# A router whose second phase starts one step early, with a new table of pauses and one code per token

## The chip, the cores and the metric

The kernel runs on one core of a Trainium2 chip. The metric is device time in microseconds (us) of one execution. Below, PE is TensorE (matmuls), DVE is VectorE, ACT is ScalarE, POOL is GpSimd, and SP is SyncE, which here issues transfers and reads a register.

## What is computed

Three stages follow one another on 2304 tokens of width 512: causal attention mixed with a small memory (4 batches, 8 heads, 576 positions, 64 wide), a mixture of 8 experts, and a dense layer with the activation h * tanh(softplus(h)). The change lies in the second stage, and what runs beside it. Cut to what matters:

```
def moe(x, w_gate, w1, w2):               # x [2304, 512], E = 8, cap = 288
    logits = x @ w_gate                   # [2304, 8]
    order = argsort(-logits.flatten())
    assigned[:] = -1; counts[:] = 0
    for idx in order:                     # greedy, largest logit first
        tok, e = idx // E, idx % E
        if assigned[tok] >= 0 or counts[e] >= cap:
            continue
        assigned[tok] = e; counts[e] += 1
    for e in range(E):
        mask = assigned == e
        out[mask] = maximum(x[mask] @ w1[e], 0) @ w2[e]

def dense(x, w_in, w_out):                # 512 -> 2048 -> 512
    h = x @ w_in
    return (h * tanh(softplus(h))) @ w_out
```

## The kernel before

**The router.** The greedy assignment is sequential over 18432 logits, but only eight times does an expert fill up. So the router (class `Router`) works in eight phases. In a phase every token that is still free looks at its best expert that is not full, and a search finds the largest threshold at which some expert fills up. That expert's 288 tokens are then final. The order in which experts fill is the order in which they are computed: "expert k" in this document is the one that phase k closes, and its number is known to the program only at run time (`eid`).

The search (method `search`) fixes the threshold in six steps of 5 or 6 bits. In a step DVE compares every token's best logit with 32 or 64 candidate thresholds (tile `cm`), 18 small matmuls count the tokens of each expert above each threshold (PE `rt<-oh,cm`, L715; `oh` is a one-hot of each token's best expert), DVE turns the counts into an indicator (`ge`, `ind`), and one more matmul adds the indicators up, the vote (PE `rt<-ind,ones`, L730). After the search come a count per expert (L608), the number of the expert (`em`, `eid`), a 0/1 mark of its tokens (`bt`, with a matmul at L637), each token's place in the expert's list (L647, L648), and, in three pieces, the list of token numbers (DVE `ohp`, PE L676, then `idx`). After phase 0 the matmul engine has nothing but the router to do until the first tokens are there.

**The experts.** For expert k, three indirect transfers issued by POOL fetch its 288 rows (`xg<-xd,idx`, L993), 12 matmuls against the identity turn them (L1005), and ACT and DVE split them into a high and a low half (`xt`, L1012 and L1014). Then come the matmuls at L1021: each product is made in three passes (high x high, low x high, high x low), and the matrices are 288 tokens wide. `h<-xt,wf` and `acc<-act,wf` are the expert's two layers, `h<-y,wa` and `acc<-act,wb` the first half of the dense layer for the same tokens. Expert weights are streamed: SP loads 256 KB pieces (`raw<-moe_w`) once `eid` is known, ACT rounds each (L952, L954), and a POOL transfer that adds completes the low half (`wf<-raw`, L960). There are 5 buffers of raw pieces and 7 of finished ones. The second half of the dense layer, for all experts, comes after the last phase.

**What sets the order.** The order of instructions on PE and on POOL is the order in which the program issues them. DVE, ACT and SP are ordered by a scheduler in the compiler. The program issues the matmuls of the experts from a list (`plan`), and at places between groups of 6 or 12 matmuls calls `slot()`. A slot advances each of several background generators by one step: the router (`routing`), the loads, the gathers (`tokens`), the evacuations. A generator that yields n is called again after n slots. `Router.wait(i)` looks that n up in the table `WAIT`; entry 1 is the pause between a step's comparison and its matmuls, entry 0 that before the vote, entry 3 that before the matmul on `bt`, entry 5 that between the pieces of the list. The third row is used while the router is not further than two phases ahead of the expert being computed (`done <= cur + X["AH"]`); in the order as built, phase k+2 runs while expert k or k+1 is computed, so that row is the one in force.

`tokens(k)` issues the gather as soon as phase k is done and the tokens before it are turned, then lets `X["TW"]` = 18 slots pass and turns in four pieces with pauses between. When the plan comes to expert k first (`up1` sets `hold`), the pauses are skipped and what is left is turned at once. Phase 1 may not begin before the first group of expert 0 has been issued (`while k and not done1[0]`).

Of the kernel before, what the change touches and what calls it, by code (L numbers as in the profile page):

```python
# [466 lines left out]
NEG = -1.0e30  # L467
STEPS = ((64, 26), (64, 20), (32, 15), (32, 10), (32, 5), (32, 0))

WAIT = ((1, 2, 2, 3, 1, 4), (1, 3, 2, 2, 1, 3), (1, 1, 2, 2, 1, 2))  # L470
NTOK, E, CAP, NJ = 2304, 8, 288, 18
G, GP = 3, 96

# [71 lines left out]
class Router:  # L545
# [3 lines left out]
    def __init__(self, tc, C, cp, rp, ps, L):  # L549
        self.nc, self.C, self.rp, self.ps, self.L = tc.nc, C, rp, ps, L  # L550
        self.tc = tc
        nc = self.nc
        self.crow = cp.tile([128, E], F32, name="crow")
        nc.vector.memset(self.crow, float(CAP))
        self.pen = cp.tile([128, NJ], F32, name="pen")
        nc.vector.memset(self.pen, 0.0)
        self.A = cp.tile([128, NJ, E], BF, name="Aoh")
        nc.vector.memset(self.A, 0.0)
        self.idx = cp.tile([GP, E, G], I32, name="idx")
        self.eid = cp.tile([128, E], I32, name="eid")  # L560
        self.known = self.done = self.busy = 0
        self.mark, self.cur = None, 0

    def wait(self, i):
        return WAIT[2 if self.done <= self.cur + X["AH"] else self.busy][i]

    def after(self):

# [4 lines left out]

    def phase(self, k):
        nc, C, rp = self.nc, self.C, self.rp
        L, pen, crow, A = self.L, self.pen, self.crow, self.A
        last = k == E - 1
        bj = lambda a, n: a[:, :, None].to_broadcast([128, a.shape[1], n])
        m = rp.tile([128, NJ], F32, name="m")
# [5 lines left out]
        mu = rp.tile([128, NJ], F32, name="mu")  # L585
# [3 lines left out]
        mx = rp.tile([128, NJ], F32, name="mx")  # L589
        nc.vector.tensor_reduce(mx, w, axis=AX.X, op=OP.max)  # L590
        oh = rp.tile([128, NJ, E], BF, name="oh")
        nc.vector.tensor_tensor(oh, w, bj(mx, E), op=OP.is_equal)
        yield 1
        gg = rp.tile([128, 2, NJ], BF, name="gg")
        if last:
            for a in range(2):
                nc.vector.tensor_scalar(gg[:, a], mu, NEG / 2, None, op0=OP.is_ge)
        else:
            cut = yield from self.search(mu, oh)
            for a, op in enumerate((OP.is_ge, OP.is_gt)):  # L600
                nc.vector.tensor_scalar(gg[:, a], mu, cut, None, op0=op)

        Z = rp.tile([128, 2, NJ, E], BF, name="Z")
        for a in range(2):
            nc.vector.tensor_tensor(Z[:, 1 - a], oh, bj(gg[:, a], E), op=OP.mult)
        yield self.wait(2)
        p = self.mm()
        nc.tensor.matmul(p[:, 0:2 * NJ * E], C["ones"], Z.rearrange("p a j e -> p (a j e)"), start=True, stop=True)  # L608

        nc.vector.tensor_add(A, A, Z[:, 0])  # L610
        yield 1
        cnt = rp.tile([128, 2, E], F32, name="cnt")
        nc.vector.tensor_reduce(cnt, p[:, 0:2 * NJ * E].rearrange("p (a j e) -> p a e j", a=2, j=NJ),
                                axis=AX.X, op=OP.add)
        nc.vector.tensor_sub(Z[:, 1], Z[:, 1], Z[:, 0])
        es = rp.tile([128, E], F32, name="es")
        em = rp.tile([128, 1], F32, name="em")
        nc.vector.tensor_tensor(es, cnt[:, 1], crow, op=OP.is_ge)
        yield 1
        nc.vector.tensor_sub(crow, crow, cnt[:, 0])  # L620
        nc.vector.tensor_tensor(es, es, C["pref"], op=OP.mult)
        nc.vector.tensor_reduce(em, es, axis=AX.X, op=OP.max)
        nc.vector.tensor_scalar(es, es, em, None, op0=OP.is_equal)
        nc.vector.tensor_scalar(self.eid[:, k:k + 1], em, -1.0, float(E), op0=OP.mult, op1=OP.add)
        self.known = k + 1
        yield 1
        q = rp.tile([128, 2, NJ, E], BF, name="q2")
        eb = es[:, None, :].to_broadcast([128, NJ, E])
        nc.vector.tensor_tensor(q[:, 0], A, eb, op=OP.mult)
        nc.vector.tensor_tensor(q[:, 1], Z[:, 1], eb, op=OP.mult)  # L630
        yield 1
        bt = rp.tile([128, 2 * NJ], BF, name="bt")
        with nc.allow_low_precision("sums of one-hot entries"):
            nc.vector.tensor_reduce(bt, q.rearrange("p a j e -> p (a j) e"), axis=AX.X, op=OP.add)
        yield self.wait(3)
        p = self.mm()
        nc.tensor.matmul(p[0:36, 0:128], bt, C["ones"], start=True, stop=True)  # L637
# [8 lines left out]
        p = self.mm()  # L646
# [20 lines left out]
        p = None  # L667
        for c in range(4):
# [4 lines left out]
            if c:  # L673
                p = p or self.mm()
                for j in range(6 * c - 6, 6 * c):
# [6 lines left out]
                                                   op1=OP.add)  # L682
# [11 lines left out]
    def search(self, mu, oh):  # L694

        nc, C, rp = self.nc, self.C, self.rp
        cut = t = None
        for s, (T, sh) in enumerate(STEPS):
# [9 lines left out]
            for c in range(parts):  # L708
                j = slice(n * c, n * c + n)
# [18 lines left out]
            yield self.wait(0)  # L728
            p = self.mm()
            nc.tensor.matmul(p[:, 0:1], C["ones"][0:T, :], ind[0:T], start=True, stop=True)  # L730
            yield 1
            t = rp.tile([128, 1], I32, name="xt", bufs=2)
            if s == 0:
# [80 lines left out]
def moe(tc, ctx, C, xd, L, w1, w2, w32, whl, convert, out):  # L814
# [43 lines left out]
    def until(cond):  # L858
        while not cond():
            slot()  # L860
# [257 lines left out]

    def routing():
        for k in range(E):  # L1120
            while k and not done1[0]:
                yield 1
            yield from R.phase(k)

# [11 lines left out]

    def up1(k, f):
        until(lambda: R.done > k)
        hold[0] = ROUTE
        until(lambda: k in xts)  # L1140
        x = xts[k].get()
        hold[0] = None
        hs[k, f] = up(weight("wf", (k, 0, f)), x, relu)
        used["wf"] += 1
        done1[0] += 1
        slot()
# [67 lines left out]

    downs, ys, gs, fetched = {}, {}, {}, {}
    for u, c, k, f in plan:
        R.busy, R.cur = int(c > 1), k
# [27 lines left out]

X = {"MO": ("PE", "Pool"), "P": 4, "P0": 4, "L1": 2, "RX": 0, "XB": 2, "LAG": 6, "TW": 18, "TS": 2, "LD": 8,
     "LG": 2, "RAWB": 5, "WFB": 7, "ACTB": 12, "GB": 7, "NG": 4, "CL": (0, 1.5, 1, 2, 3, 4), "C0": 2,
     "CW": 2, "FW": 3, "FE": 4, "AH": 2, "PE": 300, "PR": 300, "PC": 600}


def program(tc, q, k, v, M_prev, z_prev, beta, w_gate, w1, w2, w_in, w_out, out):
# [54 lines left out]
```

## Time and profile before

| | us |
|---|---|
| median of 3 runs (lowest to highest) | 1119.19 (1118.27 to 1119.87) |
| the profiled execution, its own time | 1112.46 |
| its span, first to last instruction | 1110.7 |
| PE busy | 1006.2 (91% of the span) |
| DVE busy | 655.5 (59%) |
| ACT busy | 680.6 (61%) |
| POOL busy | 343.9 (31%) |

The median is 0.6% above the profiled execution; the rows below are all from that execution. Attention takes the first 307 us, phase 0 of the router the next 30, the seven other phases run beside the experts until about 740 us, and from there on the dense layer runs alone. A busy share is an average over these stages. Idle time on an engine matters where PE waits for it.

### The profile page before, as it was taken

The numbers are of one execution on the slowest core, as the hardware profiler recorded it, in microseconds if no ns is written. First come the engines' busy times: TensorE is split into PE (matmuls) and PEld (weight loads), VectorE is DVE, ScalarE is ACT, GpSimd is POOL, SyncE is SP. The second block draws the span as 40 slices with busy tenths as digits, with TensorE's granted clock in tenths as the row PEclk, the third lists the DMA queues.
The fourth block names the chain that finished last, engine by engine and source line by source line (L and its number), as shares of the span: only waits on it lengthen the run. The fifth ranks groups of instructions, "written<-read, shape, count | busy, mean of one in ns | idle before, by whom it ended". The sixth has DMA issues, their size and how long they took to land.

```text
span 1110.7 us, 22438 instructions
## 1 busy us (share of the span) xinstructions
PE 1006.2 (91%) x8088; PEld 930.1 (84%) x8088; DVE 655.5 (59%) x1986; ACT 680.6 (61%) x1632; POOL 343.9 (31%) x468
## 2 busy tenths in 40 slices
PE   5999899999926969989899987899999999999995
PEld 4778788788815969878888987899999999999995
DVE  6887878776563565665684765666652543333332
ACT  5576667677504583654755846648473976666662
POOL 5677566675204232404223334220000001111112
PEclk9899999999956979989899999999999999999998
DMA  7889988897099876958939949565536312222201
GB/s 172 218 208 235 241 204 218 227 237 184 19 331 205 197 183 168 223 131 188 232 100 229 232 99 229 169 170 174 171 98 209 125 65 86 87 86 86 76 23 43
DMA packets 177488, 182.61 MB, mean 164 GB/s; under 512 B 90912, under 2 KB 131904, under 8 KB 175328
## 3 DMA queue, kind: packets, MB, share of 16 engines
q1 hardware_dynamic: 157152, 134.59, 42.3%
q0 software_dynamic: 20224, 46.58, 19.4%
q8 instruction: 64, 1.05, 0.4%
q14 instruction: 48, 0.39, 0.1%
HBM read 97.17 MB, written 36.18 MB: 120 GB/s over the span
## 4 chain that ended last, share of the span: by engine, by line
PE 65%; DVE 10%; ACT 9%; DMA 9%; issue 3%; SPq 1%; POOL 1%; POOLq 0%; ACTq 0%; DVEq 0%
PE acc L1021 22%; PE h L1021 22%; PE o L367 4%; DMA raw<-moe_w 3%; PE pt L341 3%; DMA wf<-raw 2%; PE s L309 2%; PE o L390 2%; PE o L359 2%; PE rt L715 2%; PE s L313 2%; ACT L1095 2%; PE o L363 1%; ACT U L1095 1%; DVE H L1099 1%
## 5 line engine op out<-in xcount | busy, mean ns | idle before, releaser
L1021 PE MATMUL acc<-act,wb 128*128 128x288 f32 x1536 | 236.1, 304 | 2.3 <-DVE act L1102 2.3
L1021 PEld LDWEIGHTS acc<-act,wb 128*128 128x128 f32 x1536 | 217.5, 193 | 4.1 <-DVE act L1102 3.7
L1099 DVE TENSOR_TENSOR H<-H,U 128x288 f32<-128x288 f32 x128 | 57.0, 455 | 160.5 <-ACT U L1095 160.4
L960 POOL DMA_DIRECT2D wf<-raw x93 | 82.3, 912 | 219.4 <-ACT wf L954 122.6
L952 ACT CAST wf<-raw 128x512 fp32r<-128x512 f32 x128 | 79.1, 618 | 85.5 <-DMA raw<-moe_w 65.9
L1021 PE MATMUL h<-xt,wf 128*128 128x288 f32 x768 | 124.4, 309 | 3.4 <-DVE xt L1014 3.4
L1021 PE MATMUL acc<-act,wf 128*128 128x288 f32 x768 | 119.9, 307 | 0.0
L1021 PEld LDWEIGHTS h<-xt,wf 128*128 128x128 f32 x768 | 110.7, 197 | 9.6 <-issue 5.0
L1021 PE MATMUL h<-xt,wa 128*128 128x288 f32 x768 | 114.2, 297 | 1.3 <-DVE wa L963 1.0
L1021 PE MATMUL h<-y,wa 128*128 128x288 f32 x768 | 114.6, 302 | 0.0
L1188 POOL DMA_INDIRECT out<-xg,idx x24 | 24.3, 1011 | 288.0 <-ACT xg L1185 287.4
L1021 PEld LDWEIGHTS acc<-act,wf 128*128 128x128 f32 x768 | 108.4, 194 | 2.0 <-issue 1.4
L1021 PEld LDWEIGHTS h<-y,wa 128*128 128x128 f32 x768 | 105.8, 191 | 3.6 <-issue 3.0
L1021 PEld LDWEIGHTS h<-xt,wa 128*128 128x128 f32 x768 | 105.3, 188 | 2.5 <-DVE wa L963 1.6
L1086 ACT ACTIVATE U<-h 128x288 f32<-128x288 f32 x128 | 53.2, 416 | 81.2 <-PE h L1021 79.8
L342 ACT COPY T<-pt 128x512 f32<-128x512 f32 (+3 forms) x128 | 57.6, 455 | 63.4 <-PE pt L341 62.8
L325 ACT ACTIVATE P<-s,nm 128x576 f32<-128x576 f32 (+4 forms) x160 | 84.2, 535 | 8.1 <-DVE nm L323 6.2
L1062 ACT ACTIVATE act<-h 128x288 fp32r<-128x288 f32 x64 | 26.0, 406 | 103.0 <-PE h L1021 102.1
L341 PE MATMUL pt<-ident,P 128*128 128x128 f32 x400 | 70.4, 283 | 0.6 <-DVE T L342 0.3
L1064 DVE SCALAR_TENSOR_TENSOR act<-h,act 128x288 fp32r<-128x288 f32 x64 | 29.0, 454 | 63.9 <-ACT act L1062 60.7
L367 PE MATMUL o<-T,vm 128*64 128x128 f32 x640 | 64.9, 290 | 0.0
L309 PE MATMUL s<-k,q 128*128 128x288 f32 (+3 forms) x192 | 60.1, 350 | 2.4 <-ACT P L325 1.4
(237 smaller groups left out, 2058.2 us busy)
## 6 DMA issues: line engine op xcount, KB each, us to landing
raw<-moe_w SPq DMA_DIRECT2D x128, 256.0 KB, 4.3
wf<-raw POOLq DMA_DIRECT2D x93, 256.0 KB
k<-kh SPq DMA_DIRECT2D x60, 160.0 KB, 3.7
yd<-y SPq DMA_DIRECT2D x8, 1152.0 KB, 8.0
xt<-yd SPq DMA_DIRECT2D x8, 1152.0 KB, 5.2
whl<-parts SPq DMA_DIRECT2D x16, 512.0 KB, 5.5
part<-o SPq DMA_DIRECT2D x8, 576.0 KB, 4.0
wf<-part SPq DMA_DIRECT2D x16, 288.0 KB, 3.2
```

The source lines that it names most:

```text
L309: nc.tensor.matmul(vw[h][:, a:e], q1[:, h, r], k1[:, h, kb[h] + a:kb[h] + e], start=True, stop=False, skip_group_check=True)
L325: nc.scalar.activation(P[:, h * w:(h + 1) * w], vw[h][:, 0:w], AF.Exp, bias=nm[:, h:h + 1], scale=1.0, accum_out=den[:, h:h + 1])
L341: nc.tensor.transpose(t[:, j * 128:(j + 1) * 128], P[:, (c + j) * 128:(c + j + 1) * 128], ident)
L342: (nc.scalar.copy if eng else nc.vector.tensor_copy)(T[:, c:c + m], t[:, 0:m * 128].rearrange("p (a b) -> p a b", b=128))
L367: nc.tensor.matmul(o[s, 0:n], vm[:, j - 1 if h else 4 - j, h, :], T[:, i + j if h else i - j, 0:n], start=False, stop=(j == i), skip_group ...
L952: nc.scalar.copy(dst[:, 0], t)
L960: nc.gpsimd.dma_start(dst[:, 1].bitcast(F32), t, accum_op=OP.add)
L1021: nc.tensor.matmul(p, w[:, a, c * 128:(c + 1) * 128], x(b), start=first and i == 0, stop=last and i == 2)
L1064: nc.vector.scalar_tensor_tensor(h.t[:, 1], p[:, 0:CAP], 0.0, h.t[:, 0], op0=OP.max, op1=OP.subtract)
L1086: s = nc.scalar.activation(U, p[:, 0:CAP], AF.Sigmoid, scale=-1.0)
L1095: s = nc.scalar.activation(U, U, AF.Sin, scale=-2.0, bias=half_pi[:, 0:1])
L1099: nc.vector.tensor_mul(H, H, U)
```

## The change

Three things are changed. Phase 1 of the router may be issued without waiting for expert 0, and expert 0 waits until phase 1 has cast its first vote (a new counter, `votes`). The table of pauses has two rows instead of three, chosen by the number of finished phases alone. And tokens carry a code (the best expert's preference number, in `at`) that is compared once with the chosen expert's, where one-hot rows of 8 were multiplied and summed (`A`, `Z`, `q`).

```
-WAIT = ((1, 2, 2, 3, 1, 4), (1, 3, 2, 2, 1, 3), (1, 1, 2, 2, 1, 2))
+WAIT = ((1, 2, 2, 2, 1, 3), (1, 1, 2, 2, 1, 2))
...
     def wait(self, i):
-        return WAIT[2 if self.done <= self.cur + X["AH"] else self.busy][i]
+        return WAIT[self.done <= 1][i]
...
-            for a, op in enumerate((OP.is_ge, OP.is_gt)):
-                nc.vector.tensor_scalar(gg[:, a], mu, cut, None, op0=op)
         Z = rp.tile([128, 2, NJ, E], BF, name="Z")
-        for a in range(2):
-            nc.vector.tensor_tensor(Z[:, 1 - a], oh, bj(gg[:, a], E), op=OP.mult)
+        ops = (OP.is_ge, OP.is_ge if last else OP.is_gt)
+        for a, op in enumerate(ops):
+            nc.vector.scalar_tensor_tensor(Z[:, 1 - a], bj(mu, E), cut, oh, op0=op, op1=OP.mult)
         yield self.wait(2)
         p = self.mm()
         nc.tensor.matmul(p[:, 0:2 * NJ * E], C["ones"], Z.rearrange("p a j e -> p (a j e)"), start=True, stop=True)
-        nc.vector.tensor_add(A, A, Z[:, 0])
+        for a, op in enumerate(ops):
+            nc.vector.tensor_scalar(gg[:, a], mu, cut, None, op0=op)
+        nc.vector.tensor_mul(sure, gg[:, 1], mx)
+        nc.vector.tensor_mul(at[:, 1], gg[:, 0], mx)
+        nc.vector.tensor_sub(at[:, 1], at[:, 1], sure)
+        nc.vector.tensor_add(at[:, 0], at[:, 0], sure)
...
-        nc.vector.tensor_sub(Z[:, 1], Z[:, 1], Z[:, 0])
...
+        nc.vector.tensor_scalar(bt, at.rearrange("p a j -> p (a j)"), em, None, op0=OP.is_equal)
...
-        yield 1
-        nc.vector.tensor_tensor(q[:, 0], A, eb, op=OP.mult)
-        nc.vector.tensor_tensor(q[:, 1], Z[:, 1], eb, op=OP.mult)
-        yield 1
-            nc.vector.tensor_reduce(bt, q.rearrange("p a j e -> p (a j) e"), axis=AX.X, op=OP.add)
         yield self.wait(3)
...
             nc.tensor.matmul(p[:, 0:1], C["ones"][0:T, :], ind[0:T], start=True, stop=True)
+            self.votes += 1
...
     def routing():
         for k in range(E):
-            while k and not done1[0]:
+            while k > 1 and not done1[0]:
                 yield 1
             yield from R.phase(k)
...
     def up1(k, f):
         until(lambda: R.done > k)
+        if (k, f) == (0, 0):
+            until(lambda: R.votes > len(STEPS))
         hold[0] = ROUTE
```

Three places on PE show what this moves. **Where expert 0 begins.** Before, PE's rows from the last piece of phase 0's list (L676) on:

```order
L676 LDWEIGHTS ohp
L676 MATMUL rt<-gc,ohp 96x6
L676 LDWEIGHTS ohp
L676 MATMUL rt<-gc,ohp 96x6
L1005 MATMUL h<-ident_63,xg 128x96 x12
L1021 MATMUL h<-xt,wf 128x288 x36
L715 LDWEIGHTS cm
```

After, at the same place (L714 is the old L715, L729 the vote): the last two of the 18 matmuls of phase 1's first step, its vote, then the tokens.

```order
L714 LDWEIGHTS cm
L714 MATMUL rt<-oh,cm 64x8
L714 LDWEIGHTS cm
L714 MATMUL rt<-oh,cm 64x8
L729 LDWEIGHTS ones
L729 MATMUL rt<-ind,ones 128x1
L1005 MATMUL h<-ident_63,xg 128x96 x12
L1021 MATMUL h<-xt,wf 128x288 x18
L714 LDWEIGHTS cm
```

One step has moved in front of the turning of expert 0's tokens, and the second step stands after 18 matmuls of expert 0 where the first stood after 36.

**Where expert 1 begins.** Before, from the last matmul of phase 1's list (L676) to the turning of expert 1's tokens (L1005):

```order
L676 MATMUL rt<-gc,ohp 96x6
L1021 MATMUL acc<-act,wb 128x288 x6
L1021 MATMUL h<-y,wa 128x288 x12
L1021 MATMUL acc<-act,wb 128x288 x12
L1005 MATMUL h<-ident_63,xg 128x96 x12
L1021 MATMUL h<-xt,wf 128x288 x12
L715 LDWEIGHTS cm
```

After, the rows behind the same last matmul (now L675) of phase 1:

```order
L675 MATMUL rt<-gc,ohp 96x6
L675 LDWEIGHTS ohp
L675 MATMUL rt<-gc,ohp 96x6
L1021 MATMUL h<-y,wa 128x288 x48
L714 LDWEIGHTS cm
```

and, behind that step of phase 2, the rows up to its next step:

```order
L1021 MATMUL h<-y,wa 128x288 x6
L1021 MATMUL acc<-act,wb 128x288 x6
L729 LDWEIGHTS ones
L729 MATMUL rt<-ind,ones 128x1
L1021 MATMUL acc<-act,wb 128x288 x6
L1021 MATMUL h<-y,wa 128x288 x12
L1021 MATMUL acc<-act,wb 128x288 x6
```

then 18 matmuls of that next step, 6 of `acc<-act,wb`, and the turning of the tokens. So 30 matmuls stood between the end of phase 1 and the turning of expert 1's tokens, and now 48 + 6 + 6 + 6 + 12 + 6 + 6 = 90 do, with two router steps.

**Where expert 4 begins.** After the change, from the end of a step of phase 5:

```order
L714 MATMUL rt<-oh,cm 32x8
L1021 MATMUL acc<-act,wf 128x288 x6
L1005 MATMUL h<-ident_63,xg 128x96 x12
L1021 MATMUL h<-xt,wf 128x288 x6
L729 LDWEIGHTS ones
L729 MATMUL rt<-ind,ones 128x1
L1021 MATMUL h<-xt,wf 128x288 x6
```

Before, expert 4's 12 turning matmuls stood in four groups of 3 with matmuls between; now they are one block, 90 matmuls behind the end of phase 4. Expert 5's are one block too (102 behind). Expert 2's, which were a group of 3 and a block of 9 before, are four groups of 3 now.

## Rows read from the trace of the kernel before

**Rows 1.** The page: PE's busy tenths and granted clock in 40 slices.

```profile
PE   5999899999926969989899987899999999999995
PEclk9899999999956979989899999999999999999998
```

**Rows 2.** Windows, 400 to 412 us: busy time by engine, granted clock, DMA.

```profile
400.00:412.00 12.00, 4.63 (x23) 3.37 (x22) 7.58 (x21) 10.97 (x24) 8.87 (x10) 0.72 0.98 209
```

**Rows 3.** PE's waits, 336 us to the end: total us, times, longest.

```profile
PE rt L676 <- DVE ohp L671: 10.6, 3, 6.4
PE h L1005 <- DMA xg<-xd,idx: 9.1, 5, 4.5
PE rt L730 <- DVE ind L727: 8.3, 6, 3.7
...
PE rt L637 <- DVE bt L634: 3.9, 4, 2.0
PE h L1021 <- DVE xt L1014: 3.4, 2, 2.8
PE rt L715 <- DVE oh L592: 3.4, 1, 3.4
PE rt L715 <- DVE cm L710: 2.4, 4, 1.3
```

**Rows 4.** PE's timeline where expert 1 begins: start, us, what, idle before.

```profile
396.68 0.39 PE L676 MATMUL rt<-gc,ohp 128*96 128x6 bf16 x6
...
399.39 1.78 PE L1021 MATMUL acc<-act,wb 128*128 128x288 f32 x12
405.67 0.39 PE L1005 MATMUL h<-ident,xg 96*128 96x96 f32 x1 [4.50 <-DMA xg<-xd,idx]
408.37 0.42 PE L1005 MATMUL h<-ident,xg 96*128 96x96 f32 x1 [2.31 <-DMA xg<-xd,idx]
409.33 2.15 PE L1005 MATMUL h<-ident,xg 96*128 96x96 f32 x10 [0.54 <-DMA xg<-xd,idx]
411.46 3.25 PE L1021 MATMUL h<-xt,wf 128*128 128x288 f32 x12
...
415.69 3.25 PE L1021 MATMUL acc<-act,wb 128*128 128x288 f32 x12
```

**Rows 5.** PE's timeline: a first step of phase 0, and expert 0's turning.

```profile
310.11 1.12 PE L715 MATMUL rt<-oh,cm 128*64 128x8 bf16 x18 [4.48 <-DVE oh L592]
...
341.48 0.39 PE L1005 MATMUL h<-ident,xg 96*128 96x96 f32 x1 [5.02 <-issue]
...
344.02 2.14 PE L1005 MATMUL h<-ident,xg 96*128 96x96 f32 x10 [0.96 <-DMA xg<-xd,idx]
```

**Rows 6.** DVE's timeline in phase 0, from the expert's number to its mark.

```profile
328.75 0.16 DVE L622 TENSOR_REDUCE em<-es 128x1 f32<-128x8 f32 x1
...
329.78 0.45 DVE L634 TENSOR_REDUCE bt<-q 128x36 bf16<-128x288 bf16 x1
```

**Rows 7.** PE's timeline where expert 2 begins.

```profile
485.53 0.91 PE L1005 MATMUL h<-ident,xg 96*128 96x96 f32 x9
489.20 1.06 PE L1021 MATMUL h<-xt,wf 128*128 128x288 f32 x6 [2.76 <-DVE xt L1014]
...
491.61 1.64 PE L1021 MATMUL acc<-act,wb 128*128 128x288 f32 x6
```

**Rows 8.** ACT and DVE near 527 us, and shares of the waiting chain, 336 to 740.

```profile
526.92 0.62 ACT L952 CAST wf<-raw 128x512 fp32r<-128x512 f32 x1 [4.28 <-DMA raw<-moe_w]
...
528.40 0.46 DVE L1064 SCALAR_TENSOR_TENSOR act<-h,act 128x288 fp32r<-128x288 f32 x1 [6.98 <-ACT act L1062]
...
by line: PE acc L1021 22.8%; PE h L1021 21.9%; DMA raw<-moe_w 9.3%; DMA wf<-raw 6.8%; PE rt L715 3.5%; issue 3.4%; DVE H L1099 3.0%; ACT L1095 2.9%; ACT wf L952 1.7%; ACT wf L954 1.6%; ACT U L1095 1.5%; ACT U L1086 1.5%; DVE ohp L671 1.4%; 
```

**Rows 9.** Windows over two gather instructions of POOL, columns as in rows 2.

```profile
635.79:641.34 5.55, 3.68 (x28) 3.45 (x26) 5.40 (x15) 5.17 (x12) 5.55 (x1) 1.00 0.34 101
337.87:341.81 3.94, 0.33 (x1) 0.18 (x1) 1.73 (x4) 0.00 (x0) 3.33 (x4) 0.50 0.30 86
```

More of the change, by code (lines that the diff above doesn't have):

```diff
@@ L556, in __init__ @@
         nc.vector.memset(self.pen, 0.0)
-        self.A = cp.tile([128, NJ, E], BF, name="Aoh")
-        nc.vector.memset(self.A, 0.0)
+        self.at = cp.tile([128, 2, NJ], F32, name="at")
+        nc.vector.memset(self.at, 0.0)
         self.idx = cp.tile([GP, E, G], I32, name="idx")
         self.eid = cp.tile([128, E], I32, name="eid")
-        self.known = self.done = self.busy = 0
-        self.mark, self.cur = None, 0
+        self.known = self.done = 0
+        self.votes = 0
+        self.mark = None
     def wait(self, i):
-        return WAIT[2 if self.done <= self.cur + X["AH"] else self.busy][i]
+        return WAIT[self.done <= 1][i]
     def after(self):
@@ L575, in phase @@
         nc, C, rp = self.nc, self.C, self.rp
-        L, pen, crow, A = self.L, self.pen, self.crow, self.A
+        L, pen, crow, at = self.L, self.pen, self.crow, self.at
         last = k == E - 1
@@ L593, in phase @@
         yield 1
-        gg = rp.tile([128, 2, NJ], BF, name="gg")
-        if last:
-            for a in range(2):
-                nc.vector.tensor_scalar(gg[:, a], mu, NEG / 2, None, op0=OP.is_ge)
-        else:
+        cut = NEG / 2
+        if not last:
             cut = yield from self.search(mu, oh)
-            for a, op in enumerate((OP.is_ge, OP.is_gt)):
-                nc.vector.tensor_scalar(gg[:, a], mu, cut, None, op0=op)
         Z = rp.tile([128, 2, NJ, E], BF, name="Z")
-        for a in range(2):
-            nc.vector.tensor_tensor(Z[:, 1 - a], oh, bj(gg[:, a], E), op=OP.mult)
+        ops = (OP.is_ge, OP.is_ge if last else OP.is_gt)
+        for a, op in enumerate(ops):
+            nc.vector.scalar_tensor_tensor(Z[:, 1 - a], bj(mu, E), cut, oh, op0=op, op1=OP.mult)
+        gg = rp.tile([128, 2, NJ], F32, name="gg")
         yield self.wait(2)
@@ L608, in phase @@
         nc.tensor.matmul(p[:, 0:2 * NJ * E], C["ones"], Z.rearrange("p a j e -> p (a j e)"), start=True, stop=True)
-        nc.vector.tensor_add(A, A, Z[:, 0])
+        for a, op in enumerate(ops):
+            nc.vector.tensor_scalar(gg[:, a], mu, cut, None, op0=op)
+        sure = rp.tile([128, NJ], F32, name="sure")
+        nc.vector.tensor_mul(sure, gg[:, 1], mx)
+        nc.vector.tensor_mul(at[:, 1], gg[:, 0], mx)
+        nc.vector.tensor_sub(at[:, 1], at[:, 1], sure)
+        nc.vector.tensor_add(at[:, 0], at[:, 0], sure)
         yield 1
@@ L619, in phase @@
         yield 1
-        nc.vector.tensor_sub(crow, crow, cnt[:, 0])
         nc.vector.tensor_tensor(es, es, C["pref"], op=OP.mult)
         nc.vector.tensor_reduce(em, es, axis=AX.X, op=OP.max)
-        nc.vector.tensor_scalar(es, es, em, None, op0=OP.is_equal)
+        bt = rp.tile([128, 2 * NJ], BF, name="bt")
+        nc.vector.tensor_scalar(bt, at.rearrange("p a j -> p (a j)"), em, None, op0=OP.is_equal)
         nc.vector.tensor_scalar(self.eid[:, k:k + 1], em, -1.0, float(E), op0=OP.mult, op1=OP.add)
         self.known = k + 1
-        yield 1
-        q = rp.tile([128, 2, NJ, E], BF, name="q2")
+        nc.vector.tensor_sub(crow, crow, cnt[:, 0])
         eb = es[:, None, :].to_broadcast([128, NJ, E])
-        nc.vector.tensor_tensor(q[:, 0], A, eb, op=OP.mult)
-        nc.vector.tensor_tensor(q[:, 1], Z[:, 1], eb, op=OP.mult)
-        yield 1
-        bt = rp.tile([128, 2 * NJ], BF, name="bt")
-        with nc.allow_low_precision("sums of one-hot entries"):
-            nc.vector.tensor_reduce(bt, q.rearrange("p a j e -> p (a j) e"), axis=AX.X, op=OP.add)
+        nc.vector.tensor_scalar(es, es, em, None, op0=OP.is_equal)
         yield self.wait(3)
@@ L1216, in moe @@
     for u, c, k, f in plan:
-        R.busy, R.cur = int(c > 1), k
         if u == "up" and c == 1:
@@ L1247 @@
      "LG": 2, "RAWB": 5, "WFB": 7, "ACTB": 12, "GB": 7, "NG": 4, "CL": (0, 1.5, 1, 2, 3, 4), "C0": 2,
-     "CW": 2, "FW": 3, "FE": 4, "AH": 2, "PE": 300, "PR": 300, "PC": 600}
+     "CW": 2, "FW": 3, "FE": 4, "PE": 300, "PR": 300, "PC": 600}
 def program(tc, q, k, v, M_prev, z_prev, beta, w_gate, w1, w2, w_in, w_out, out):
```

## The prediction, made before the changed kernel ran

> **What bounds the kernel now.** I read the page first, then PE's waits, then the timeline at the longest of them. In the 40 slices of the page [rows 1] PE is at 9 or 8 tenths nearly everywhere; the holes are in slices 12 to 15 (about 305 to 416 us) and then single 9s that turn to 7 or 8 up to slice 26 (about 740 us). Behind that PE is full, so nothing that the router does can help or hurt there except by moving the start. The granted clock dips in the same slices. The table of PE's waits from 336 us on [rows 3] says who ends these holes: almost all are the router's own small matmuls waiting for DVE (10.6 for the list, 8.3 for votes, 3.9 for the mark `bt`, 2.4 and 3.4 for comparisons), the gather (9.1), and freshly turned tokens (3.4). PE is in program order, so each such wait stops the experts' matmuls behind it. Each has a second price: after a long hole PE runs at 1.2 instead of 2.4 GHz for a while. Where expert 1 begins [rows 4], 12 matmuls took 1.78 us before the hole (0.148 each) and 3.25, twice in a row, after it.
>
> **The change part by part.** The sum is made against the profiled execution's own 1112.46 us.
>
> *Codes.* In phase 0 PE idles, so DVE's chain counts. `em` ends at 328.91 and `bt` starts at 329.78 with 0.45 to run [rows 6]; the new `bt` is one comparison over 36 elements directly behind `em`, which I price between 0.16 (the 8-element row) and 0.45: up to 1.1 us saved. But `eid` does not come sooner, so expert 0's weight pieces do not either, and the chain of waits from 336 to 740 us gives 16.1% of its time, 65 us, to the transfers `raw` and `wf` [rows 8]. I credit nothing; bounds 1.1 saved to 0. The two products for `Z` become two fused operations of the same size; the four short operations on `at` stand behind the issue of the matmul whose result DVE waits for anyway: 0.
>
> *The first step.* It now runs between the end of phase 0 and expert 0's tokens. PE stood idle 5.02 us there, and the last third of the gather came only with the row at 344.02, 2.5 us after the first [rows 5]. The 18 matmuls took 1.12 us in phase 0 at the low clock [rows 5], and the vote behind them waits for DVE about as long again: 2.2 us inside 7.5. Cost 0; if DVE were late by the whole cover, +2. It also leaves expert 0, where PE was busy, worth at most its 1.12; with the weight stream above I credit 0.
>
> *Expert 1's tokens.* Phase 1 now ends 60 matmuls sooner against the work. From the end of its list (396.68 + 0.39) to the row in which the last third is there (409.33) are 12.3 us [rows 4]; the 90 matmuls that now stand between cover 90 x 0.148 = 13.3 us, and two router steps come on top. So the three holes, 4.50 + 2.31 + 0.54 = 7.35 us [rows 4], go. With them goes the low clock: twice 3.25 - 1.78 = 2.94, and ten turning matmuls in 2.15 where nine took 0.91 at full clock [rows 7], 1.1. Together 11.4. What is late next: at full speed the first matmul on the new tokens stands right behind the 12 turning ones, and must wait until ACT and DVE have copied them out. That is the case of expert 2 now: 2.76 us of wait, then six matmuls in 1.06 and six in 1.64 instead of 0.89 [rows 7], 3.7 in all. Expert 1's copies share ACT with the activation of expert 0, as expert 2's did with that of expert 1, so I take the same 3.7. Net -7.7; bounds -11.4 (no wait) to -4.0 (twice that wait).
>
> *Expert 2's tokens* are spread over four groups now, so their 3.7 us go: -3.7, or 0 if the last group meets the same queue.
>
> *Experts 4 and 5* get the block of 12 that expert 2 loses. Beside them runs only the first layer's simple activation, so I take 1.5 us each; below, two passes like the 0.46 us row of DVE [rows 8], 0.9; above, the 3.7 of expert 2. Sum +3.0 (1.8 to 7.4). The gathers are 90 and 102 matmuls old by then, 13.3 us or more.
>
> *Longer pauses.* In phases 2 to 7 each comparison has one more slot before its matmuls, and so has each piece of the list; in the order a slot is 6 matmuls or 12, at least 6 x 0.148 = 0.89 us of cover. From the waits [rows 3]: comparisons 2.4 in four, the longest 1.3, leave 0.4 (-2.0); the one for `oh`, 3.4, loses 0.9; the list's three, 10.6, lose 0.9 each (-2.7); the mark's four, 3.9, longest 2.0, lose up to 1.1 each by the shorter chain and leave 0.9 (-3.0); votes keep their 8.3, since their pause is unchanged. Sum -8.6. Two waits over 1 us vanish or nearly so, and with each the 1.47 us of 12 slow matmuls [rows 4]: -2.9. Together -11.5. I take half, -5.7, because many of these waits come from elsewhere. At 526.92 ACT waited 4.28 us for a weight piece, DVE behind it 6.98 for ACT [rows 8], and the router's vote stood in DVE's queue; such a delay finds another router step if it misses this one. Bounds -11.5 to 0. A phase grows by 36 matmuls (252 to 288 in the order), 5.3 us. Nothing waits for that: expert 4's number, the tightest behind expert 1's, is known 168 matmuls, 25 us, before its tokens are turned (216 before).
>
> Sum: 0 + 0 - 7.7 - 3.7 + 3.0 - 5.7 = -14.1 us, 1098.4 for an execution like the profiled one. The runs' median is 1119.19, 6.7 above it, and I set the same difference against the median: **1105**.
>
> **The rivals.**
>
> *The weight stream sets the pace.* If the 65 us of transfers in the chain [rows 8] are the true limit from 336 to 740, PE's waits only change their name. For it: DMA engines were busy 0.98 of the window at expert 1 [rows 2]. Against it: in that window PE waited for the gather, and none of the long waits in the table is for a weight piece [rows 3]. Then what is left is about a third of the 11.4 us: -4, 1115.
>
> *Gathers come late.* The gather needs POOL to write out its transfers. One such instruction took 5.55 us, and DVE was busy 5.40 of them; three together took 3.94 where DVE was busy 1.73 [rows 9]. The changed kernel gathers for expert 1 while DVE takes phase 2's first step and turns them at the first moment. A gather longer by the difference to a usual one of about 1 us, 4.5, needs 16.8 us at expert 1 against 13.3 and two steps of 0.6 or more: PE waits 2.3 and the low clock costs 2.9 again. At experts 1, 4 and 5 that is 3 x 5.2 = 15.6, which cancels the gain: 1121. It decides when a gather takes longer than 14.5 us. The Trainium skill, "SBUF — State Buffer", section "Who interferes with whom", has a rule for this: GpSimd and one kind of VectorE operation (copies, casts and tensor-scalar forms in their two-port mode) exclude each other for a whole instruction, so the transfers that GpSimd issues wait. [...] Against it: seven of the eight gathers before had no hole of this size except expert 1's, and the 5.55 us one was not waited for at all [rows 3].
>
> *Slower: more weight pieces meet a router step.* The place is phases 3 to 7: ACT waits for a late piece, DVE for ACT, PE for the router. Two of PE's waits are of this kind and size, 3.7 and 6.4 [rows 3], and with 1.5 to 2.9 of low clock each costs about 7. Longer phases spread the router over more of the stage in which pieces arrive: 36 matmuls in 252 more chances, and the expert's number is known later from phase 4 on. Two more such meetings cancel the 14.1; with four more the time is 1119 + 14 = 1133. Against it: the added slots are cover for just these steps.
>
> **How the numbers follow.** 0.70 for the forecast, whose own range is 1095 to 1114 (the bounds above, not all at one end); 0.13 for the weight stream; 0.07 for late gathers; 0.10 for slower. A difference under 0.2%, 2.2 us, can hardly be told from none here. Faster: nearly all of the first two, 0.81. Same: 0.07, from late gathers and the ends of the others. Slower: 0.12. The range 1093 to 1118 leaves out the slower case and a low tail of about 0.07.
>
> **What would show it.** In the changed profile: no wait for the gather at expert 1, and no matmuls at 0.27 us after it, but a wait of 2 to 4 us for `xt`; blocks of 12 at experts 4 and 5 followed by waits of 1 to 2; the turning row that now stands at 344.02 within 1.5 us of that place; the wait on `bt` under 1 us in total; list and comparison waits down by a third to a half, votes as before. It would be wrong if the waits on votes grow past 15 us, if gather waits show up at experts 4 and 5, or if PE waits for weight pieces by name.

## The result, and the profile after

The changed kernel took 1128.38 us (median of 4 runs, 1126.16 to 1136.47) against 1118.93 for the kernel before on the same chip: ratio 1.0107, interval 1.0070 to 1.0144 (the two medians by themselves give 1.0084). It is 1.1% slower; I had forecast 1.3% faster. Its profiled execution took 1126.79 us, 14.3 above that of before (1112.46).

The page, PE's busy tenths and granted clock in 40 slices, against [rows 1]:

```profile
PE   5999899999827889899897898879999999999995
PEclk9899999999957989999798999989999999999998
```

Slice 15, where expert 1 begins, is an 8 now and was a 6; but some 9s have become 8s and 7s on either side of it (and four other slices rose), and there is a new 7 in slice 27 (731 to 759 us), where before had a 9. PE's waits from 336 us to the end (total us, times, longest), against [rows 3]:

```profile
PE h L1005 <- DMA xg<-xd,idx: 11.8, 6, 4.5
PE h L1005 <- DVE xt L1014: 11.7, 3, 6.6
PE rt L729 <- DVE ind L726: 5.5, 5, 2.7
PE h L1005 <- ACT H L1089: 3.9, 2, 2.3
...
PE rt L675 <- DVE ohp L670: 3.3, 2, 2.5
PE rt L714 <- DVE oh L595: 3.2, 1, 3.2
PE rt L714 <- DVE cm L709: 3.0, 4, 1.7
PE rt L636 <- DVE eid L629: 2.8, 1, 2.8
```

The router's waits did fall: its list (`ohp`) from 10.6 to 3.3, its votes (`ind`) from 8.3 to 5.5. What rose is the turning of tokens, L1005: waits for the gather, for `xt` and for ACT add up to 27.4 us, where 14.1 stood before: the gather's 9.1, and the 5.02 of idle time at expert 0's turning [rows 5] where the first step now stands.

**Expert 1** (timeline of PE after), against [rows 4]:

```profile
406.64 1.20 PE L1005 MATMUL h<-ident,xg 96*128 96x96 f32 x9
411.65 0.74 PE L1005 MATMUL h<-ident,xg 96*128 96x96 f32 x3 [3.82 <-DVE xt L1014]
413.34 1.81 PE L1021 MATMUL h<-xt,wf 128*128 128x288 f32 x6 [0.94 <-DVE xt L1014]
```

The gather is hidden, as forecast, but expert 1's matmuls begin at 413.34 instead of 411.46.

**Expert 7.** Matched matmul for matmul, the two traces swing by -9.5 to +11.0 us against each other and are level again at the experts' 2016th matmul (738.1 before, 738.7 after). Forty-eight matmuls later the changed kernel is 14.4 us behind. Windows of 736 to 770 us (columns as in [rows 2]), first before, then after:

```profile
736.00:770.00 34.00, 34.00 (x261) 34.00 (x259) 22.90 (x46) 23.30 (x49) 3.09 (x6) 1.00 0.72 220
```

```profile
736.00:770.00 34.00, 25.63 (x187) 25.04 (x185) 15.22 (x31) 13.01 (x29) 6.66 (x8) 0.85 0.59 159
```

PE after, then POOL after, in that stretch:

```profile
743.24 0.41 PE L1005 MATMUL h<-ident,xg 96*128 96x96 f32 x3
748.10 0.27 PE L1005 MATMUL h<-ident,xg 96*128 96x96 f32 x1 [4.45 <-DMA xg<-xd,idx]
750.94 0.42 PE L1005 MATMUL h<-ident,xg 96*128 96x96 f32 x1 [2.56 <-DMA xg<-xd,idx]
752.72 0.42 PE L1005 MATMUL h<-ident,xg 96*128 96x96 f32 x1 [1.36 <-DMA xg<-xd,idx]
752.85 3.23 PE L1021 MATMUL h<-xt,wf 128*128 128x288 f32 x12
```

```profile
743.93 1.01 POOL L993 DMA_INDIRECT xg<-xd,idx  x1 [0.40 <-PE h L1005]
745.24 1.06 POOL L993 DMA_INDIRECT xg<-xd,idx  x1 [0.30 <-issue]
746.61 1.44 POOL L993 DMA_INDIRECT xg<-xd,idx  x1 [0.30 <-issue]
```

The three turnings at 743.24 are expert 6's last piece; the next three are already expert 7's. Its gather begins at 743.93, and nothing stands between it and the turning that needs it: PE waits 4.45 + 2.56 + 1.36 = 8.4 us and then runs slow matmuls (12 in 3.23 us). The program says why. Phase 7 now ends 84 matmuls later (at 2034 of the experts' matmuls; before at 1950). Six matmuls on, at 2040, the plan stands in `up1(6, 0)`, waiting for expert 6's tokens with `hold` set. In `tokens` the turning pause is skipped whenever `hold` is set, for whichever expert. So expert 7's tokens were gathered and turned at once, although the plan had asked for expert 6's.

### The profile page after: what moved, and what is told of

It is laid out like the page before. It is cut to its first block, busy times and chain, and to the rows that moved or that the text cites. A ratio compares the mean times of both kernels' runs of the same rounds, so it can differ in the third digit from the quotient of the medians.

```text
span 1125.0 us, 22443 instructions
## 1 busy us (share of the span) xinstructions
PE 1009.8 (90%) x8088; PEld 930.2 (83%) x8088; DVE 649.3 (58%) x1983; ACT 681.6 (61%) x1635; POOL 342.9 (30%) x471
## 4 chain that ended last, share of the span: by engine, by line
PE 63%; DMA 11%; ACT 10%; DVE 9%; issue 4%; SPq 2%; POOL 1%; POOLq 0%; ACTq 0%; DVEq 0%
PE h L1021 22%; PE acc L1021 21%; DMA raw<-moe_w 5%; PE o L367 4%; PE pt L341 3%; DMA wf<-raw 2%; PE o L390 2%; PE o L359 2%; PE s L309 2%; PE s L313 2%; ACT L1095 1%; PE o L363 1%; PE rt L714 1%; ACT U L1095 1%; DVE H L1099 1%
## 5 line engine op out<-in xcount | busy, mean ns | idle before, releaser
L1021 PE MATMUL acc<-act,wb 128*128 128x288 f32 x1536 | 231.8, 301 | 0.7 <-DVE act L1102 0.5
L1021 PEld LDWEIGHTS acc<-act,wb 128*128 128x128 f32 x1536 | 214.2, 190 | 2.5 <-DVE act L1102 1.5
L960 POOL DMA_DIRECT2D wf<-raw x96 | 84.9, 949 | 240.5 <-ACT wf L954 136.3
L1021 PE MATMUL h<-y,wa 128*128 128x288 f32 x768 | 120.7, 313 | 3.9 <-ACT H L1089 2.1
L1021 PEld LDWEIGHTS h<-xt,wf 128*128 128x128 f32 x768 | 112.1, 199 | 10.6 <-DVE xt L1014 5.0
L1021 PEld LDWEIGHTS h<-y,wa 128*128 128x128 f32 x768 | 111.0, 200 | 8.6 <-ACT H L1089 4.8
```

The lines of the kernel that those rows point to most:

```text
L960: nc.gpsimd.dma_start(dst[:, 1].bitcast(F32), t, accum_op=OP.add)
L1021: nc.tensor.matmul(p, w[:, a, c * 128:(c + 1) * 128], x(b), start=first and i == 0, stop=last and i == 2)
```

## The experiments

Ratios are to the kernel before on the same chip. The executions of that kernel spread from 1110.77 to 1125.25 us on one chip, so I rest verdicts on the ratios, and use traces for where waits stand. Four kernels (the pause of 10 slots, the short list pause, the codes alone, and the codes with their slots and short pauses) ran on another chip than the rest.

**1. Is it the hold?** Only the expert that the plan waits for cuts the pause short:

```
-            if hold[0] is None:
+            if hold[0] is None or want[0] != k:
                 yield 1
...
-        hold[0] = ROUTE
+        hold[0], want[0] = ROUTE, k
```

> The changed kernel, with one thing altered: the pause between a gather and the turning of its tokens is cut short only while the plan waits for that very expert, not while it waits for another. In PE's order this moves only expert 7's turning, from directly behind expert 6's to 108 matmuls later; experts 0 to 6 stay as they are. Theory M (the loss is made at expert 7: its gather is issued and its turning stands right behind it on PE, 8.4 us of wait in the trace and about 5 us of matmuls at the low clock after it): about 13 us less than the changed kernel, near 1115 us, level with or a little under the kernel before. Theory R (longer pauses push the whole router late, and expert 7 is only where it shows; the time would be lost on weights or later waits anyway): at most 4 us less, 1124 or more.

Measured 1.0015 (0.9983 to 1.0046). Expert 7 is turned 108 matmuls later, and the only gather that PE waits for is expert 0's (2.9 us). So this hole cost 0.9%, some 10 us. But the rest is not the 0.987 that I had forecast.

**2. The parts.** First, short pauses in the changed kernel (*mended hold* below means the edit just shown; it is in a kernel only where the text says so):

```
-WAIT = ((1, 2, 2, 2, 1, 3), (1, 1, 2, 2, 1, 2))
+WAIT = ((1, 1, 2, 2, 1, 2), (1, 1, 2, 2, 1, 2))
```

> The changed kernel with the short pauses (1, 1, 2, 2, 1, 2) in every phase, the row that was in force in the kernel before; the early first step and the codes stay. Phases become shorter (234 to 240 matmuls in place of 288 to 336), expert 7's phase ends long before it is needed, and the turnings of experts 4 and 5 are four groups again. Theory M: the hole at expert 7 (13 us) goes, and the 6.6 us wait behind the block of expert 4 too; what the longer pauses gave back on list and comparison waits, some 6 us at most, is lost: 1108 to 1116. Theory R also says faster than the changed kernel, by 10 or more. If the longer pauses had been a gain, as the prediction had it, this run would lose against e1_own_hold by about 6 us.

Measured 0.9932 (0.9907 to 0.9958). Then the kernel before with the early step alone:

```
-            while k and not done1[0]:
+            while k > 1 and not done1[0]:
...
         until(lambda: R.done > k)
+        if (k, f) == (0, 0):
+            until(lambda: R.votes > len(STEPS))
```

> The kernel before with the early first step of phase 1 alone (old pauses, one-hots). The 7.35 us of gather wait at expert 1 and the low clock behind it, 11.4 us by the prediction, should shrink to a wait of about 4 to 5 us for copies of the turned tokens: 4 to 8 us faster than before, 1111 to 1115. If the block at expert 1 costs as much as in the changed kernel (two waits of 3.8 and 0.9 us, then slow matmuls) and PE loses as much on the list of phase 1, then no change: 1117 to 1120.

Measured 0.9844 (0.9811 to 0.9878). Then the kernel before with the new table and its rule (`self.done <= 1`) alone:

> The kernel before with the new table of pauses alone. Phases grow from 252 to 342 matmuls; phase 4 ends exactly where expert 4 is turned, phase 5 six matmuls before expert 5. Both theories: gathers are no longer covered at experts 4 and 5 and partly at 6, about 11 us each (wait and low clock, as at expert 1 before): 1140 or more, 20 to 35 us slower than before. If the prediction's view of the pauses (cover for the router's waits, -5.7) were right in sign, it would be no slower than 1120.

Measured 1.0224 (1.0199 to 1.0250). The early step alone is a gain, and the longer pauses alone, which I had priced at -5.7 us, are a loss of 25 us. With pauses alone phase 4 ends at matmul 1308, just where the plan first asks for expert 4's tokens, and PE waits for the whole gather (over all experts its waits for gathers add up to 33.7 us). PE there:

```profile
604.84 0.39 PE L676 MATMUL rt<-gc,ohp 128*96 128x6 bf16 x6
614.36 0.42 PE L1005 MATMUL h<-ident,xg 96*128 96x96 f32 x1 [9.12 <-DMA xg<-xd,idx]
615.90 0.42 PE L1005 MATMUL h<-ident,xg 96*128 96x96 f32 x1 [1.12 <-DMA xg<-xd,idx]
617.59 2.15 PE L1005 MATMUL h<-ident,xg 96*128 96x96 f32 x10 [1.28 <-DMA xg<-xd,idx]
```

**3. Is the rest the turning in blocks?** At expert 4 the changed kernel, too, turns late. Its pause (18 slots of 6 matmuls = 108) is longer than the 90 matmuls between phase 4's end and the first use, so `hold` ends it and the tokens are turned in one block. PE, ACT and DVE after:

```profile
603.49 0.91 PE L1005 MATMUL h<-ident,xg 96*128 96x96 f32 x9
610.98 0.74 PE L1005 MATMUL h<-ident,xg 96*128 96x96 f32 x3 [6.58 <-DVE xt L1014]
```

```profile
605.85 0.62 ACT L952 CAST wf<-raw 128x512 fp32r<-128x512 f32 x1 [4.54 <-DMA raw<-moe_w]
...
609.19 0.64 ACT L787 ACTIVATE cvr<-raw 128x512 f32<-128x512 uint16 x1
609.74 0.99 ACT L1012 CAST xt<-h 128x288 fp32r<-128x288 f32 x3
```

```profile
609.86 0.69 DVE L798 TENSOR_TENSOR cvr<-cvr,cve 128x512 f32<-128x512 f32 x1 [5.50 <-ACT cvr L787]
```

ACT waits 4.54 us for a weight piece, the copies of the turned tokens stand behind it in ACT's order, DVE waits for ACT, and PE for both. Two kernels with the mended hold turn sooner. The first leaves only the last two pieces together at the first use, the second has all four apart:

```
-... "LAG": 6, "TW": 18, "TS": 2 ...
+... "LAG": 6, "TW": 10, "TS": 2 ...
```

> The changed kernel with the hold that ends the turning pause for its own expert only, and that pause 10 slots instead of 18: experts 4 and 5 are turned in pieces over 24 to 36 matmuls ahead of their first use instead of in a block of 12 (waits of 6.6 and 1.3 us there). If the blocks are what is left of the loss (1.0015 with the hold alone), 0.992 to 0.996. If longer phases cost wherever turnings stand, 1.000 to 1.003. If 66 matmuls (9.8 us) are too short a cover for a gather, waits of 1 to 4 us on xg at experts 2, 3, 6 and 7 and 1.005 or more.

Measured 1.0021 (0.9993 to 1.0049). And with the pause of 18, but that between the list's pieces short again:

```
-WAIT = ((1, 2, 2, 2, 1, 3), (1, 1, 2, 2, 1, 2))
+WAIT = ((1, 2, 2, 2, 1, 2), (1, 1, 2, 2, 1, 2))
```

> The changed kernel with the same hold and the list's pause back at 2 slots, the comparisons' pause still at 2: phases end 36 to 90 matmuls sooner, expert 4 begins to turn 30 matmuls before its use, expert 5 wholly ahead of it. If turnings that come too late are the loss, 0.992 to 0.996, no wait over 2 us on xt at expert 4 or 5. If the longer comparison pause itself is the loss, 1.000 to 1.003.

Measured 1.0037 (1.0014 to 1.0060). My theory of the blocks fell. With the short list pause no wait over 2 us is left at the turnings of experts 4 and 5, and nothing is gained; its longest wait, 6.7 us, is at a list. In the kernel with 10 slots PE still waits 7.72 us for expert 4's last piece (PE, then ACT):

```profile
596.10 0.41 PE L1005 MATMUL h<-ident,xg 96*128 96x96 f32 x3
598.85 0.47 PE L1005 MATMUL h<-ident,xg 96*128 96x96 f32 x3
607.04 0.74 PE L1005 MATMUL h<-ident,xg 96*128 96x96 f32 x3 [7.72 <-DVE ge L724]
```

```profile
605.06 0.62 ACT L952 CAST wf<-raw 128x512 fp32r<-128x512 f32 x1 [6.75 <-DMA raw<-moe_w]
```

ACT waits 6.75 us for a weight piece there: two pieces meet a stall of this size just as the block of four did.

**4. Codes, and the pairs.** Codes alone; step and codes with the old table; step and pauses, and codes and pauses (these two with the mended hold); the step alone once more. The edits are the hunks of the diff shown above, taken singly.

> The kernel before with the codes alone: old table of pauses, no early first step. With step and codes but short pauses the ratio was 0.993, with the step alone 0.984, so the codes seem to cost 0.9%. If they cost by themselves (four more short DVE operations per phase, a shorter chain that brings the mark's matmul nearer), this is 1.005 to 1.010 of before. If the cost is only a matter of where phases then end against the experts (two slots per phase fewer), it is 0.997 to 1.003 here, since expert 2 to 7 are turned within 30 matmuls of where they were.

Measured 0.9987 (0.9963 to 1.0011).

> Early first step and codes with the old table of pauses; beside the step alone (0.984) only the codes differ. If the codes cost nothing of their own, as alone (0.9987), and the early step is a gain, 0.984 to 0.990. If the early step gains little and the 0.984 was a lucky order, 0.993 to 0.999, as the two kernels with step, codes and short pauses (0.993 and 0.999).

Measured 0.9972 (0.9945 to 0.9999).

> Early first step and longer pauses, old one-hots. Phases 4 and 5 end 42 matmuls (6.2 us) ahead of the first use of their experts' tokens, against a gather of 8 to 12 us from the end of the list. If lateness of the phases is what longer pauses cost, there are waits of 2 to 6 us on xg at experts 4 and 5, each with slow matmuls behind, and 1.005 to 1.015. If pauses cost or gain nothing by their lateness, 0.984 to 0.990 as the step alone.

Measured 1.0222 (1.0167 to 1.0276), above what I expected of lateness; at expert 4 its gather holes are 3.17, 1.47 and 0.48 us, and its gather waits over all experts are 12.0 us.

> Codes and longer pauses with the hold for its own expert, the first step where it was. Phases 4 and 5 end 42 and 54 matmuls ahead of the first use. By lateness: waits on xg at experts 4 and 5, 1.005 to 1.018, below the 1.022 of pauses alone, whose phases 4 and 5 end 0 and 6 matmuls ahead. If the early step is what decides, 1.015 to 1.022.

Measured 1.0112 (1.0073 to 1.0151), with 15.1 us of gather waits.

> The early first step alone once more, beside the three above on one chip, since it had few runs: 0.981 to 0.988 if the gain is real and belongs to this order of instructions; 0.993 or more if it does not hold.

Measured 0.9875 (0.9833 to 0.9917). The new table slows each of the four kernels to which it is added: from 1 to 1.0224, from 0.9844 and 0.9875 to 1.0222, from 0.9987 to 1.0112, and from 0.9972 to 1.0015 (mended hold in the last three; the intervals of the last pair overlap). The gain of the step, in turn, depends on what stands beside it: 14 to 17 us alone, none that shows beside the codes (0.9987 to 0.9972) or beside the table (1.0224 to 1.0222).

**5. Codes: DVE's work or PE's order?** Codes cost nothing alone, but 1.0 to 1.3% beside the step. They also take two one-slot pauses out of each phase. So I put them back beside step and codes, which gives PE the order of the step alone, row for row:

```
         self.known = k + 1
+        yield 1
...
         nc.vector.tensor_scalar(es, es, em, None, op0=OP.is_equal)
+        yield 1
         yield self.wait(3)
```

> Early step and codes with the old table and the two one-slot pauses put back: PE's order is that of the early step alone, row for row, and only DVE's operations differ. If the codes' DVE operations cost the 1.0% between step alone (0.984, 0.9875) and step with codes (0.9972), 0.995 to 0.999. If it was the order, 0.983 to 0.989.

Measured 0.9821 (0.9794 to 0.9847), the best of all, at 1098.48 us; I call it the *kept slots* below. The converse is the step with the old one-hots, but without the two pauses, which gives PE the order of step and codes (*lost slots*):

```
         self.known = k + 1
-        yield 1
...
         nc.vector.tensor_tensor(q[:, 1], Z[:, 1], eb, op=OP.mult)
-        yield 1
```

> Early step with the old one-hots, but without two one-slot pauses per phase: PE's order is that of step with codes, row for row. If the order decides, 0.994 to 1.000 as step with codes, or a little more because the mark's matmul now waits longer for the one-hots' chain; if the DVE operations of the codes decide, 0.983 to 0.989.

Measured 1.0019 (1.0002 to 1.0036). The order decides: the codes' own work costs nothing (if anything it gains, 1.0019 to 0.9972 in the one order, 0.9844 and 0.9875 to 0.9821 in the other), and beside the step and the old table two slots per phase cost 1.4 to 1.8% (0.9821 to 0.9972; 0.9844 and 0.9875 to 1.0019). Without the step the codes, which take the same two slots, cost nothing (0.9987). A kernel like that of the kept slots in all but the table, with short pauses throughout (that of the first diff under 2), had run before:

> Early step, codes and short pauses, with the two one-slot pauses put back that the codes took out (18 to 24 matmuls per phase). PE's order is then that of the early step alone up to expert 5, and only the DVE operations differ. If the codes' cost comes from the lost slots, 0.984 as the step alone; if from the DVE operations themselves, 0.993 as with short pauses.

Measured 0.9992 (0.9964 to 1.0020). Its order leaves that of the kept slots only from phase 5 on, whose end moves from 1422 to 1398. So the old table's short row was not in force throughout, as I had described it: from phase 5 on the longer rows count too. And *shorter* pauses lost 1.7% there (the two kernels ran on different chips), while with the slots gone they lost nothing (0.9972 to 0.9932): there is no rule that long or short is better.

**6. Is the step's gain a lucky meeting?** `"TW": 17` for 18, in the kernel before and in the step alone:

> The kernel before with the turning pause 17 slots instead of 18, which moves the turnings of experts 2 to 7 by 6 to 12 matmuls and nothing else: a change without a purpose. If the gain of the early step is one of the order's accidents, differences of this size, 0.3 to 1.0% to either side, come from such a change too; if orders are that alike, 0.998 to 1.002.

Measured 0.9983 (0.9961 to 1.0006).

> The early step alone with the same move of the turnings. If its gain comes from the step and expert 1, which the move does not touch, 0.983 to 0.989. If it hangs on one lucky meeting in phases 5 and 6, where its trace gains 8 us, anything from 0.984 to 0.998.

Measured 0.9841 (0.9814 to 0.9867). A small move of the turnings changes little on either side. The gain belongs to where the router's steps stand.

## Where the time lies

The gain of the step does not lie at expert 1. First matmuls of expert 0, before and after, then for the second run of the step alone (its lines are one further) with the start of expert 1:

```profile
346.76 6.84 PE L1021 MATMUL h<-xt,wf 128*128 128x288 f32 x36 [0.59 <-DVE xt L1014]
```

```profile
347.11 4.69 PE L1021 MATMUL h<-xt,wf 128*128 128x288 f32 x18 [0.96 <-DVE xt L1014]
```

```profile
348.55 4.19 PE L1022 MATMUL h<-xt,wf 128*128 128x288 f32 x18 [0.96 <-DVE xt L1015]
...
413.25 0.62 PE L1006 MATMUL h<-ident,xg 96*128 96x96 f32 x3 [2.87 <-DVE xt L1015]
413.98 1.81 PE L1022 MATMUL h<-xt,wf 128*128 128x288 f32 x6
```

From the one to the other: 64.70 us before (411.46 in [rows 4]), 66.23 after, 65.43 with the step alone. What was won at the gather was lost in expert 0. Its first matmuls ran slower for longer (18 in 4.69 and 4.19 us, where before 36 took 6.84), but after 192 of them the changed kernel was only 0.3 us behind. Then it came to the list of phase 1, which stands 60 matmuls sooner than before and now had to be waited for, with slow matmuls behind it (after):

```profile
385.90 0.43 PE L675 MATMUL rt<-gc,ohp 128*96 128x6 bf16 x6 [2.50 <-DVE ohp L670]
386.19 2.78 PE L1021 MATMUL h<-y,wa 128*128 128x288 f32 x12
```

After 216 matmuls it was 5.1 us behind. In the step alone it was a vote of phase 1 that was late, and after 72 matmuls that kernel was 5.0 behind:

```profile
357.23 0.16 PE L730 MATMUL rt<-ind,ones 64*128 64x1 bf16 x1 [2.04 <-DVE ind L727]
```

The step's gain lies in phases 6 and 7. From the experts' 1728th to their 2016th matmul the kernel before took 57.7 us, the second run of the step alone 47.0, the kept slots 47.3 (with 17 slots: 57.5 and 47.4; the lost slots 56.1). The trace of the kept slots gains about as much again in other stages (411.5 us from expert 0's first matmul to the 2304th, against 422.6 with the step alone and 431.3 before); I have not traced those. In the kernel before the list of phase 6 is waited for. PE, DVE and ACT before:

```profile
694.16 0.64 PE L676 MATMUL rt<-gc,ohp 128*96 128x6 bf16 x6 [6.41 <-DVE ohp L671]
694.66 3.23 PE L1021 MATMUL h<-y,wa 128*128 128x288 f32 x12
```

```profile
687.60 0.46 DVE L1064 SCALAR_TENSOR_TENSOR act<-h,act 128x288 fp32r<-128x288 f32 x1 [4.85 <-ACT act L1062]
...
692.02 2.09 DVE L671 TENSOR_TENSOR ohp<-pl,i 128x576 bf16<-128x576 bf16 x3
```

```profile
685.08 0.62 ACT L952 CAST wf<-raw 128x512 fp32r<-128x512 f32 x1 [4.80 <-DMA raw<-moe_w]
```

ACT waited 4.80 us for a weight piece, DVE 4.85 for ACT, and the list's chain of small operations stood behind that in DVE's order, between the copies for the dense layer (`y`). With the kept slots the list comes first (DVE, then ACT):

```profile
677.34 1.42 DVE L672 TENSOR_TENSOR ohp<-pl,i 128x576 bf16<-128x576 bf16 x2
...
683.26 0.46 DVE L1066 SCALAR_TENSOR_TENSOR act<-h,act 128x288 fp32r<-128x288 f32 x1 [3.31 <-ACT act L1064]
```

```profile
680.74 0.62 ACT L954 CAST wf<-raw 128x512 fp32r<-128x512 f32 x1 [3.62 <-DMA raw<-moe_w]
```

The late piece (3.62) and the stall of DVE (3.31) are there too, but the list does not stand behind them. The longest of PE's waits from 675 to 717 us there:

```profile
PE h L1023 <- ACT y L1014: 0.9, 1, 0.9
```

Counting PE's waits of over 2 us from 418 to 775 us in the timelines gives 6 in the kernel before (20.6 us in sum), 7 after (24.1), 8 with the lost slots (22.1), 3 in each run of the step alone (11.0 and 11.2), 2 with the kept slots (7.6).

## Why the prediction was wrong

A path of single edits leads from the kernel before to the changed one: early step, 0.9844 and 0.9875; codes with their slots kept, 0.9821; their slots gone, 0.9972; new table, hold mended, 1.0015; hold as it is, 1.0107. In us of 1119: -14 to -17, about -4 (the intervals overlap), +17, +5 (they overlap), +10.

This is one path of several, and the parts do not add. On top of step and table the codes with their lost slots do not cost 17 us but gain 23 (1.0222 to 1.0015, both with the mended hold): with the slots kept, phase 4 ends only 42 matmuls before expert 4's tokens are asked for, without them 90. And the table costs 5 us at the end of this path, but 25 alone and 39 to 42 right behind the step.

- **The step that failed: "A phase grows by 36 matmuls ... Nothing waits for that: expert 4's number ... is known 168 matmuls, 25 us, before its tokens are turned."** It is the step under "Longer pauses" that priced later phases at nothing. I measured cover from the expert's number. What counts is from the end of the phase to the place where the plan asks for the tokens: 156 matmuls at expert 4 before, 90 after, for a pause of 108. With the table alone none were left, PE waited 9.12 us for one gather, and the kernel was 25 us slower. And I did not ask what the plan was doing when each phase ended: at phase 7 it held for expert 6, and that alone cost 10 us. That is the rival "gathers come late" in kind, but in the changed kernel at expert 7 and through `hold`, not at experts 1, 4 and 5. It did not come through the rule of the Trainium skill ("SBUF — State Buffer", "Who interferes with whom") either: the three gather instructions took 1.01, 1.06 and 1.44 us, no long one among them, though DVE was busy with tensor-scalar forms for 1.00 us of the second. Nor does the 5.55 us row [rows 9] speak for that rule: casts and tensor-scalar forms fill only 0.57 us of it on DVE, and what made it long stays open.
- **"Longer pauses", -5.7**: the wrong sign in all four kernels that got the table, +5 (not clear of noise) to +42 us. The router's waits together did fall by 8.1 us in the trace after (29.2 to 21.1), near the -8.6 of my sum, though part of that is chance: the list's went from 10.6 to 3.3, but are 6.9 with the mended hold, whose order is the same up to expert 7. Turning waits took their place.
- **"Expert 1's tokens", -7.7**: +1.5 after. The gather's hole went and the wait of `xt` came (forecast 2 to 4 us; 3.82 + 0.94), but expert 0 took back what was won: the list of phase 1, 60 matmuls sooner, was waited for 2.50 us.
- **"Expert 2's tokens"**: its wait of 2.76 us became three at the same matmuls (0.50, 0.49 and 1.09, between 487 and 491 us), so most of the -3.7 was not won; it was not tested by itself.
- **Blocks at experts 4 and 5, +3.0**: waits of 6.58 and 1.27 in the trace. The size at expert 4 is that of a late weight piece behind which the copies stood, and without the block nothing was gained.
- **"Codes", 0**: right for DVE's work (0.9987 alone; 0.9821 against 0.9844 and 0.9875). But I counted what the codes compute, and not that two pauses go with them. Beside the step and the old table that was worth +17 us, more than the size of my whole sum; beside the new table it went the other way.
- **"The first step", 0**: right at its place; the turning row is still at 344.01. That the step alone reached the ratio that I had forecast for the whole (0.9844 and 0.9875; 0.987) is luck: it came from phases 6 and 7, where I had credited it with nothing. Of the signs that I named, votes fell (8.3 to 5.5) where I expected no change, comparisons did not fall (2.4 to 3.0), and the mark waits 2.8 where I said under 1.

Under all this lies one assumption: that a wait seen in the trace is the price of its step, and that it shrinks by the cover that one adds. In the traces shown, waits of 6.41, 6.58 and 7.72 us come from weight pieces that reach ACT late, and are paid by whichever step stands behind ACT and DVE then. I had this as the rival "more weight pieces meet a router step" and tied it to the added matmuls; the runs show that it works in both directions, and with moves that add none. What stays open is which spacing is best: the kept slots with the old table and with short pauses differ only from phase 5 on, and by 1.7% (on different chips), and I have no rule that says so beforehand.

## What to carry to other kernels

Where a program's order comes from counters and pauses, an edit that removes a pause is a move of everything behind it, and what it is worth depends on the other edits beside it; read each phase's end against the next place that asks for it, and what a flag such as `hold` is set for there. A wait whose releaser was itself waiting for a transfer belongs to the transfer and not to the step that shows it: adding cover to the step may only choose who pays. And try neutral moves, and the same order with the other work, before crediting an edit: here PE's order was worth up to 2%, the work that was saved some 0.5% at best.

## Not expected of the hardware

A late weight piece of 4.8 us stopped three engines in turn, each by its own order (ACT 4.80, DVE 4.85, PE 6.41), while the list's own three operations on DVE take 2.09. And an uncovered gather costs PE about 9 us from the first instruction (743.93 to the turning at 752.72), though the three instructions themselves take 3.5; PE's granted clock over the stretch of 736 to 770 us was 0.85, against 1.00 before.
